# Loads of x in five parts, and bulk loads held back ahead of the rows of maxima, in an attention and MLP kernel

## The chip, the cores and the metric

The kernel runs on one core of a Trainium2 chip. The core has a matrix engine (PE, with its weight loads shown apart as PEld), a vector engine (DVE), a scalar engine (ACT), GpSimd (POOL), and SyncE (SP), which here issues every DMA. The metric is the device time of one execution in microseconds, the median of several runs.

## The reference

```python
H = 32; Dh = D // H; W = 256                      # S = 2048, D = 640, F = 1536
qkv = (x @ wqkv).reshape(B, S, 3, H, Dh)          # heads of 20 columns
scores = einsum("bhqd,bhkd->bhqk", q, k) * Dh ** -0.5
mask = (idx[:, None] - idx[None, :] >= 0) & (idx[:, None] - idx[None, :] < W)
p = softmax(where(mask, scores, -1e9))
s = einsum("bhqk,bhkd->bhqd", p, v) @ wo          # attention branch
h = relu(x @ w1 + b1) ** 2
g = silu(h @ w2 + b2)                             # MLP branch
return x0 + s * g                                 # x = layernorm(x0) feeds both branches
```

All of it is float32. The kernel splits each operand of a product into a high and a low part and adds three products (high by high, high by low, low by high).

## The kernel before

There are three stages. In the first, x is normalised and transposed in four blocks of 512 rows (`BT`), each as a high and a low tile of 128 partitions by 5 x 512 numbers (five column blocks of D). Both tiles of a block are also written to memory (`xs_d`), 1,280 KB each. v and the first group of q and k are computed here.

The second stage is one loop over steps `s` at the end of the kernel, 16 head pairs by 16 tiles of 128 queries and 11 steps more. In each step a pair's scores `sps` are computed and DVE takes their maxima along the rows; nine steps later the transposed scores `stps` of the same tile are computed with the maxima subtracted, and ACT takes their exponential; two steps after that, every fourth step, `values` multiplies by v into `ops`. The maxima travel like this: every fourth step, `max_rows` transposes the maxima of four query tiles, ACT and POOL split them into a high and a low row (`row`, `mrow`), and SP issues two DMAs of 4 KB (`qs<-mrow`) that put them into two rows of the q tile `qs`. The transposed scores read these rows as part of their operand. For three groups of four out of four their first reader comes three steps after the two DMAs, for the first group of a pair five steps.

Between these, PE is filled by a generator (`filler`): first the products for q and k of the other heads (`qkps`), then the MLP in eight blocks, `hps` (x by w1) and `yps` (the squared result by w2), four blocks of x with the first half of F and four with the second. The block order is 3, 0, 1, 2 and then 2, 3, 0, 1, so six of the eight need a new x (`xb`), loaded from `xs_d` by `load_xb` when the last `hps` of the block before is issued. Each `hps` group takes its 30 products for one output column block and half of 512 rows, column block by column block, three products each. Last, the third stage multiplies by wo and writes the output.

The order on every engine is set when the kernel is built, by the code's own clock, with the engines running through their lists in order. PE runs two halves of its rows side by side (`halves`, `both`), the second a little behind the first.

All DMAs stand in SP's one list. They come into it in three ways. Stores (`o<-osb`, `y<-ysb`, `q_d`/`k_d<-shm`) are posted and go out at `post_all`, twice a step. Rows of maxima go out directly. Everything else that is large waits in lists and is handed out by `issue`, twice a step: weight pieces (`start_pieces`, `raw`), and then `bulk`, which holds the loads of q and k for the next head pair (`pair_loads`, eight of 240 KB) and those of x. Each item has a price; each call adds `RATE` = 0.9 of credit, never above 0.9, and items go out while the credit is over zero. `ensure_bulk` issues what has not gone out when its user comes: pair loads at the first step of a pair, x at the start of its block. DMAs use eight completion counters in turn, and one is issued only when the eighth before it has landed.

```python
while credit[0] > 0 and start_pieces(1):
    credit[0] -= 1.0
while bulk and credit[0] > 0:
    cost, fn = bulk.pop(0)
    fn()
    credit[0] -= cost
```

Line numbers in the profile are those of the helper that issues: L681 a bulk DMA, L564 a posted store, L503 a row of maxima, L753 a weight piece, L419 a load of v, L874 a load of `yin` (the first half's y). L468 is a half product, L478 the scores, L518 the transposed scores, L546 `ops`.

## Time and profile before

| | us |
|---|---|
| median of three runs | 883.76 |
| lowest, highest | 883.56, 889.21 |
| the profiled execution | 882.05 |
| its span, first to last instruction | 880.3 |
| stage two (first `load_v` to the last step) | about 116 to 783 |

The page gives busy times by engine, then slices of the span, the DMA queues, the chain of work that ended last, groups of instructions, and DMA issues. Of the queries, "waits" lists who waited for whom, "timeline" lists instructions in order of time (a DMA's row on SP is its issue, not its transfer), and "windows" gives the busy time of each engine in a stretch, with DMA share and GB/s. The granted PE clock is full throughout:

```
PEclk9999999999999999999999999999999999999999
DMA  7997687778788363263366255475255364165995
```

### The profile page before, as it was taken

To read this page: it belongs to the slowest core of one execution; us is meant where nothing else is said; L and a number is where in the kernel's file an instruction comes from. 1 tells how busy PE (TensorE), PEld (TensorE's weight loads), DVE (VectorE), ACT (ScalarE), POOL (GpSimd) and SP (SyncE) were. 2 spreads that over 40 slices of the span, in tenths; PEclk is the share of its full clock that TensorE was granted. 3 is DMA by queue.
4 is the path that set the end of the run, shared out by engine and by line. 5 is a ranking of instruction groups with operands and counts; after the bars stand their busy time and mean duration, and the time that the engine had idled before them with its cause. 6 is when DMAs were issued, how large, how long until landed. Compare 5 with 4: busy or idle time off the path is not lost.

```text
span 880.3 us, 26692 instructions
## 1 busy us (share of the span) xinstructions
PE 860.6 (98%) x10640; PEld 802.6 (91%) x10640; DVE 498.7 (57%) x1448; ACT 414.8 (47%) x800; POOL 329.9 (37%) x700
## 2 busy tenths in 40 slices
PE   8999999999999999999999999999999999999997
PEld 8999999888888899989989989988998989989997
DVE  7652146656567755555555676754655555354774
ACT  5222114545556744744644664743653654642231
POOL 6010002333333643534633543643543543621343
PEclk9999999999999999999999999999999999999999
DMA  7997687778788363263366255475255364165995
GB/s 269 313 394 265 179 230 256 229 249 278 240 269 297 84 223 108 60 224 96 95 207 174 73 154 145 130 223 150 76 202 161 90 209 119 52 196 183 284 299 175
DMA packets 85988, 168.59 MB, mean 192 GB/s; under 512 B 8680, under 2 KB 40552, under 8 KB 83304
## 3 DMA queue, kind: packets, MB, share of 16 engines
q1 hardware_dynamic: 85864, 166.89, 60.1%
q8 instruction: 84, 1.38, 0.7%
q14 instruction: 40, 0.33, 0.1%
HBM read 94.71 MB, written 71.57 MB: 189 GB/s over the span
## 4 chain that ended last, share of the span: by engine, by line
PE 76%; DMA 11%; ACT 4%; DVE 4%; issue 3%; POOL 2%; SPq 0%; DVEq 0%; POOLq 0%; ACTq 0%
PE yps L468 16%; PE hps L468 16%; PE qkps L468 13%; PE ops L546 8%; PE vps L228 8%; DMA qs<-mrow 5%; PE stps L518 4%; PE sps L478 4%; PE qkps L205 3%; DMA out_dram<-res 3%; POOL res L1099 2%; PE wops L599 1%; DMA ks<-k_d 1%; ACT p L524 1%; ACT relu L926 1%
## 5 line engine op out<-in xcount | busy, mean ns | idle before, releaser
L486 DVE CUSTOM_DVE_ANT_0 junk<-sps,mask 128x384 bf16<-128x384 f32 (+2 forms) x512 | 271.9, 531 | 205.0 <-PE sps L478 75.1
L524 ACT ACTIVATE p<-stps 128x768 f32<-128x768 f32 (+2 forms) x256 | 196.9, 769 | 258.0 <-PE stps L518 202.1
L468 PE MATMUL yps<-w,hh 64*128 64x320 f32 x1536 | 231.6, 310 | 4.0 <-DVE sq L931 3.0
L525 POOL TENSOR_SCALAR_AFFINE_SELECT p<-p 128x256 f32<-128x256 f32 x256 | 104.6, 409 | 332.7 <-ACT p L524 327.6
L468 PE MATMUL hps<-xb,w 64*128 64x256 f32 x2520 | 218.2, 283 | 0.0
L468 PEld LDWEIGHTS hps<-xb,w 64*128 64x128 f32 x2520 | 206.4, 187 | 5.2 <-issue 5.1
L468 PEld LDWEIGHTS yps<-w,hh 64*128 64x128 f32 x1536 | 188.8, 185 | 9.7 <-DVE sq L931 4.8
L468 PE MATMUL yps<-w,hl 64*128 64x320 f32 x768 | 182.8, 309 | 0.0
L478 PE MATMUL sps<-ks,qs 60*128 60x384 f32 (+2 forms) x512 | 139.9, 344 | 1.9 <-DVE mt L486 1.6
L518 PE MATMUL stps<-qs,ks 62*128 62x384 f32 (+2 forms) x512 | 130.1, 335 | 5.8 <-DMA qs<-mrow 5.7
L468 PEld LDWEIGHTS yps<-w,hl 64*128 64x128 f32 x768 | 121.6, 185 | 2.1 <-issue 2.1
L468 PE MATMUL qkps<-xT,wgkh 64*128 64x512 f32 x320 | 100.9, 395 | 0.0
L468 PE MATMUL qkps<-xT,wgqh 64*128 64x512 f32 x320 | 99.4, 393 | 0.0
L546 PE MATMUL ops<-p,vp 128*21 128x128 f32 (+1 forms) x2112 | 92.8, 313 | 0.0
L527 POOL TENSOR_SCALAR_AFFINE_SELECT p<-p 128x256 f32<-128x256 f32 x224 | 92.1, 411 | 0.0
L518 PEld LDWEIGHTS stps<-qs,ks 62*128 62x128 f32 x512 | 83.4, 187 | 8.7 <-issue 7.7
L478 PEld LDWEIGHTS sps<-ks,qs 60*128 60x128 f32 x512 | 84.4, 185 | 5.1 <-DVE mt L486 3.9
L546 PEld LDWEIGHTS ops<-p,vp 128*21 128x21 f32 x2112 | 65.2, 100 | 22.3 <-issue 8.8
L932 POOL TENSOR_TENSOR hl<-sq,hh 128x256 fp32r<-128x256 f32 x96 | 70.6, 736 | 27.5 <-DVE sq L931 22.9
L228 PE MATMUL vps<-wv,xT 128*128 128x320 f32 x480 | 71.5, 308 | 0.0
L228 PEld LDWEIGHTS vps<-wv,xT 128*128 128x128 f32 x480 | 70.5, 188 | 0.1
L931 DVE SCALAR_TENSOR_TENSOR sq<-hps,b1t,relu 128x256 f32<-128x256 f32 x96 | 46.2, 482 | 39.2 <-ACT relu L926 39.1
(100 smaller groups left out, 1212.1 us busy)
## 6 DMA issues: line engine op xcount, KB each, us to landing
ks<-k_d SPq DMA_DIRECT2D x64, 240.0 KB
qs<-q_d SPq DMA_DIRECT2D x64, 240.0 KB
xb<-xs SPq DMA_DIRECT2D x12, 1280.0 KB
xs<-xT SPq DMA_DIRECT2D x8, 1280.0 KB
y<-ysb SPq DMA_DIRECT2D x32, 320.0 KB
k_d<-shm SPq DMA_DIRECT2D x19, 512.0 KB
q_d<-shm SPq DMA_DIRECT2D x19, 512.0 KB
o<-osb SPq DMA_DIRECT2D x64, 128.0 KB
```

The source lines that it names most:

```text
L205: nc.tensor.matmul(ps, wt[:, c, :], xT[part][b][:, c * BT + t0:c * BT + t0 + n], start=m == 1, stop=m == 3 * KC)
L228: nc.tensor.matmul(ps, xT[xp][b][:, c * BT + t * P: c * BT + (t + 1) * P], wv[wp][:, c, nh * HALF:(nh + 1) * HALF], start=first and m == 0 ...
L468: return nc.tensor.matmul(out, a[r], b_[r], skip_group_check=True, **kw)
L478: nc.tensor.matmul(ss[hh][:, :nk], qs[i][o, q * P:(q + 1) * P], ks[i][o, k0 * P:k0 * P + nk], start=True, stop=True)
L486: nc.vector.tensor_tensor_reduce(out=junk[:, :nk], in0=ss[hh][:, :nk], in1=mask[:, 3 * P - nk:], scale=1.0, scalar=-3.0e38, op0=ALU.add, o ...
L518: nc.tensor.matmul(tps[:, hh, :n], ks[i][o, kb * P:(kb + 1) * P], qs[i][o, kb * P:kb * P + n], start=True, stop=True)
L524: nc.scalar.activation(p32[:, :, :n], tps[:, :, :n], AF.Exp, scale=SCALE)
L525: nc.gpsimd.affine_select(p32[:, :, 0:P], p32[:, :, 0:P], pattern=[[0, 2], [1, P]], compare_op=ALU.is_ge, fill=0.0, base=0, channel_multip ...
L527: nc.gpsimd.affine_select(p32[:, :, 2 * P:], p32[:, :, 2 * P:], pattern=[[0, 2], [-1, P]], compare_op=ALU.is_gt, fill=0.0, base=0, channel ...
L546: nc.tensor.matmul(ot[r0:r0 + VW, c0:c0 + len(part), :], vps[p][:, kb // 4, kb % 4, hh, :], pt[:, hh, :].rearrange("p (t n) -> p t n", n=P ...
L931: nc.vector.scalar_tensor_tensor(sq, ps.tile[:, sl], b1t[:, fi + i:fi + i + 1], r, ALU.add, ALU.mult)
L932: nc.gpsimd.tensor_sub(hh[1][:, sl], sq, f32(hh[0][:, sl]))
```

## The change

Two things. A load of x for an MLP block is cut into its five column blocks, for each of the two tiles: ten items of 256 KB at a price of 0.8 each instead of two of 1,280 KB at 1.8. And `issue` hands out nothing in a step with `s % 4 == 3`, nor in a step with `s % 4 == 0` until that step's `rows()` has been called. In four steps there are eight calls of `issue`; three of them now do nothing. The gate holds for weight pieces and for pair loads too. Posted stores and loads of v, `yin` and rows of maxima do not pass it, nor does what `ensure_bulk` or `ensure` forces out.

```diff
-    bulk = []
+    bulk, rowed = [], [False]
     credit = [0.0]
 
     def issue(amount):
+        if state[2] % 4 == 3 or state[2] % 4 == 0 and not rowed[0]:
+            return
         credit[0] = min(credit[0] + amount, amount)
...
     def load_xb(b):
         xb = [bigp.tile([P, KC * BT], F32R, tag="big", name=f"xb{p}_{b}") for p in range(2)]
-        its = [bulk_dma(1.8, f32(xb[p]), xs_d[p][b]) for p in range(2)]
+        cs = [slice(c * BT, (c + 1) * BT) for c in range(KC)]
+        its = [bulk_dma(0.8, f32(xb[p])[:, c], xs_d[p][b][:, c]) for p in range(2) for c in cs]
         return xb, its
...
         for s in range(steps):
-            state[2] = s
+            state[2], rowed[0] = s, False
...
             if rows:
                 rows()
+            rowed[0] = True
             fill((s + EARLY_FILL) * pace)
             post_all()
             issue(RATE)
```

The instructions of PE, DVE, ACT and POOL stand in the same order in both programs. SP's list has the 48 issues more, and bulk loads and weight pieces stand at other places in it. One such place, ahead of the MLP block that uses block 1 of x for the first time; before, a load of x on both sides of a row of maxima:

```order
L564 DMA o_87<-osb 2x64x256
L681 DMA xb_1_6149<-xs_1_73 128x2560
L503 DMA qs_116<-mrow 2x4x128 x2
L681 DMA xb_1_6150<-xs_1_77 128x2560
L681 DMA ks_1351<-k_d 60x1024
L681 DMA qs_1350<-q_d 60x1024
```

and now:

```order
L564 DMA o_87<-osb 2x64x256
L503 DMA qs_116<-mrow 2x4x128 x2
L683 DMA xb_1_6157<-xs_1_73 128x512 x5
L683 DMA xb_1_6158<-xs_1_77 128x512
L564 DMA o_88<-osb 2x64x256
L564 DMA y_83<-ysb 128x640
```

The row of maxima now comes first, the two tiles of x in parts behind it, and the loads of k and q later still.

## The prediction

> **What bounds it now.** I read the page first.

> ```profile
> span 880.3 us, 26692 instructions
> PE 860.6 (98%) x10640; PEld 802.6 (91%) x10640; DVE 498.7 (57%) x1448; ACT 414.8 (47%) x800; POOL 329.9 (37%) x700
> ```

> PE is idle for 880.3 - 860.6 = 19.7 us in all, and its program is the same in both kernels. A change in the order of DMAs can give back no more than those idle times that a DMA makes, and can take time only by making new ones. So the next view is the waits of PE, with total, times and longest:

> ```profile
> PE stps L518 <- DMA qs<-mrow: 5.7, 8, 1.7
> ```

> the same for its weight loads, over the whole span,

> ```profile
> PEld stps L518 <- issue: 7.7, 8, 2.0
> ```

> and over 360 to 680 us alone, where most of the loads of x for MLP blocks lie:

> ```profile
> PEld stps L518 <- issue: 6.6, 6, 2.0
> ```

> The transposed scores wait for a row of maxima eight times, 5.7 us as the matmuls show it and 7.7 us as the weight loads do. I use the second, since the pipeline drains before it stands still. Six of the eight, 6.6 us, lie where x is loaded. The longest is read in the chain of waits

> ```profile
> 578.50 10.61 DMA ks<-k_d
> 589.18 6.42 DMA qs<-mrow
> ```

> and on the weight loads' timeline:

> ```profile
> 595.66 0.21 PEld L518 LDWEIGHTS stps<-qs,ks 62*128 62x128 f32 x2 [2.01 <-issue]
> ```

> A 4 KB transfer takes 6.42 us to land, after its issue waited for a load of k that took 10.61 us. What was queued ahead is on SP's timeline:

> ```profile
> 575.22 0.41 SPq L681 DMA_DIRECT2D xb<-xs  x1
> 576.84 1.11 SPq L503 DMA_DIRECT2D qs<-mrow  x2
> 578.06 0.35 SPq L681 DMA_DIRECT2D xb<-xs  x1
> 578.50 0.39 SPq L681 DMA_DIRECT2D ks<-k_d  x1
> ...
> 579.83 0.49 SPq L681 DMA_DIRECT2D qs<-q_d  x1
> 585.25 0.52 SPq L564 DMA_DIRECT2D o<-osb  x1
> 585.87 0.42 SPq L874 DMA_DIRECT2D yin<-y  x1
> 586.35 1.14 SPq L564 DMA_DIRECT2D y<-ysb  x1
> 588.51 1.17 SPq L503 DMA_DIRECT2D qs<-mrow  x2
> ...
> 597.28 0.52 SPq L564 DMA_DIRECT2D o<-osb  x1
> 599.61 1.27 SPq L503 DMA_DIRECT2D qs<-mrow  x2
> ```

> The sizes are in the page's part 6:

> ```profile
> ks<-k_d SPq DMA_DIRECT2D x64, 240.0 KB
> ...
> xb<-xs SPq DMA_DIRECT2D x12, 1280.0 KB
> ...
> y<-ysb SPq DMA_DIRECT2D x32, 320.0 KB
> ...
> o<-osb SPq DMA_DIRECT2D x64, 128.0 KB
> ```

> Two whole loads of x, four loads of k and q, then o, yin and y, and only then the row. Second thing to see: the second row's DMA (589.18) was held until the k load of 578.50 had landed, and that is the eighth DMA ahead of it in program order; SP keeps eight in flight. The last view is the windows; the last two columns are DMA share and GB/s.

> ```profile
> 504.50:507.00 2.50, 2.01 (x29) 1.80 (x28) 1.52 (x5) 1.93 (x6) 2.14 (x5) 1.00 0.13 33
> 583.00:587.50 4.50, 3.89 (x47) 3.83 (x48) 2.60 (x9) 2.10 (x5) 0.93 (x3) 1.00 0.97 248
> 590.00:597.30 7.30, 5.56 (x82) 4.68 (x80) 2.66 (x9) 1.90 (x3) 1.58 (x5) 1.00 0.53 176
> ```

> From 583 to 587.5 us the DMA engines are full at 248 GB/s: the row waits behind bytes. In the first window only an o store moves, at 33 GB/s and a share of 0.13, some 2 of 16 engines; its 128 KB take about 3.9 us, and a row always follows an o store.

> **What the change does, part by part.** *PE, DVE, ACT and POOL* keep their order, instruction for instruction; so the operations cost nothing, and all is in SP's queue. 48 more DMA issues (six blocks by 10 for 2) at 0.41 us each are 20 us of SP, spread over 400 us in which SP mostly waits for data: nothing, except through the slots of eight in flight.

> *The row that follows a load of x.* SP before, around the stall of 2.01 us (xb_3 is x of block 3, ks and qs are the loads of k and q, vp of v, yin of the first half's y; osb, ysb and mrow are stored):

> ```order
> L681 DMA xb_3_10352<-xs_3_75 128x2560
> L503 DMA qs_1350<-mrow 2x4x128 x2
> L681 DMA xb_3_10353<-xs_3_79 128x2560
> L681 DMA ks_117<-k_d 60x1024
> L681 DMA qs_116<-q_d 60x1024
> L681 DMA ks_117<-k_d 60x1024
> L681 DMA qs_116<-q_d 60x1024
> L564 DMA o_88<-osb 2x64x256
> L874 DMA yin<-y_83 128x640
> L564 DMA y_84<-ysb 128x640
> L503 DMA qs_1350<-mrow 2x4x128 x2
> ```

> and now:

> ```order
> L503 DMA qs_1350<-mrow 2x4x128 x2
> L683 DMA xb_3_10376<-xs_3_75 128x512 x5
> L683 DMA xb_3_10377<-xs_3_79 128x512
> L564 DMA o_88<-osb 2x64x256
> L877 DMA yin<-y_83 128x640
> L564 DMA y_84<-ysb 128x640
> L503 DMA qs_1350<-mrow 2x4x128 x2
> ```

> The first row has no load of x ahead of it any more. Ahead of the second stand 6 x 256 = 1,536 KB of bulk where 2 x 1,280 + 4 x 240 = 3,520 KB stood: 2.0 MB less, at 248 GB/s 8.2 us. It was 2.01 us late. This stall goes, and the five like it, for the same move stands at all of them: -6.6 us. What is late next follows.

> *The row after that.* The bulk taken out of the first interval comes in the next. The intervals from the row of 588.51 to that of 599.61, before:

> ```order
> L503 DMA qs_1350<-mrow 2x4x128 x2
> L419 DMA vp_10605<-v_d 128x672
> L874 DMA yin<-y_83 128x640
> L564 DMA y_84<-ysb 128x640
> L564 DMA o_85<-osb 2x64x256
> L503 DMA qs_1350<-mrow 2x4x128 x2
> ```

> and now:

> ```order
> L503 DMA qs_1350<-mrow 2x4x128 x2
> L683 DMA xb_3_10377<-xs_3_79 128x512 x2
> L419 DMA vp_10631<-v_d 128x672
> L683 DMA xb_3_10377<-xs_3_79 128x512 x2
> L683 DMA ks_117<-k_d 60x1024
> L877 DMA yin<-y_83 128x640
> L564 DMA y_84<-ysb 128x640
> L683 DMA qs_116<-q_d 60x1024
> L564 DMA o_85<-osb 2x64x256
> L683 DMA ks_117<-k_d 60x1024
> L683 DMA qs_116<-q_d 60x1024
> L503 DMA qs_1350<-mrow 2x4x128 x2
> ```

> Four parts and four loads of k and q are new, 4 x 256 + 4 x 240 = 1,984 KB: 8.2 us at 248 GB/s. The window of 590 to 597.3 has 0.47 x 7.3 = 3.4 us of DMA time free, so the row lands up to 4.8 us later than now. Its first user is this:

> ```profile
> 605.25 0.19 PEld L518 LDWEIGHTS stps<-qs,ks 62*128 62x128 f32 x1
> ```

> The o store issued at 597.28 is through by about 597.28 + 3.9 = 601.2 at the earliest, the row behind it soon after, so some 3 to 4 us of slack lie before 605.25. Late by 0 to 2 us; I take 1.5, as the two loads behind the o store lie on the same engines. The same interval at its twin, some 200 us before, has no yin load: 0 to 2, I take 0.4.

> *The last part of x.* A load that went out whole is now ten items handed out at about one a turn, five turns in eight. For two of the six blocks the tenth is issued only when the block begins. SP before the sixth such block (xb_0, second time), before:

> ```order
> L503 DMA qs_1350<-mrow 2x4x128 x2
> L874 DMA yin<-y_83 128x640
> L564 DMA y_84<-ysb 128x640
> L419 DMA vp_12259<-v_d 128x672
> ```

> and now:

> ```order
> L503 DMA qs_1350<-mrow 2x4x128 x2
> L877 DMA yin<-y_83 128x640
> L564 DMA y_84<-ysb 128x640
> L683 DMA xb_0_11768<-xs_0_76 128x512
> L683 DMA ks_117<-k_d 60x1024
> ```

> The part takes the place that vp had. On SP's timeline that was here, and for the block of xb_2, where it stands the same way, here:

> ```profile
> 672.87 0.38 SPq L419 DMA_DIRECT2D vp<-v_d  x1
> ```

> ```profile
> 468.83 0.37 SPq L419 DMA_DIRECT2D vp<-v_d  x1
> ```

> The 14th weight load of each block is the first to read the last part (each of the five column blocks takes three products, the last part is the low half of the fifth):

> ```profile
> 673.87 0.19 PEld L468 LDWEIGHTS hps<-xb,w 64*128 64x128 f32 x1
> ```

> ```profile
> 470.31 0.19 PEld L468 LDWEIGHTS hps<-xb,w 64*128 64x128 f32 x1
> ```

> A load of 320 KB with nothing ahead of it, the first of the chain, takes

> ```profile
> 0.80 2.83 DMA xt<-in_A_x_dram
> ```

> Issue plus 2.83 is 675.70 and 471.66: late by 1.8 and 1.35 us. With 640 KB and 320 KB just ahead it is somewhat more: I take 2.3 and 1.7. The other end is the 10.61 us of the k load: late by 9.6 and 9.1. PE takes its instructions in order, so scores queued behind the product wait with it. The other four blocks get their tenth part at least one row of maxima before they begin.

> [...] In the trace the loads of 576 to 580 us went out within 2 us and filled the engines together (share 0.97), so smaller transfers in flight side by side still fill them. [...]

> *Weight loads* pass the same gate. The one that it brings closest to its use, the fifth of w1's second half, stood ahead of this row of maxima and now stands right behind it, at 519.0:

> ```profile
> 517.75 1.27 SPq L503 DMA_DIRECT2D qs<-mrow  x2
> ```

> ACT reads it here:

> ```profile
> 522.19 0.84 ACT L765 ACTIVATE w<-raw 128x768 fp32r<-128x768 f32 x1
> ```

> 519.0 + 2.83 = 521.85: it costs nothing by 0.3 us, and if it lands late some 0.5 us of ACT, which is busy 47% of the span.

> *The stage of q and k* (to 280 us) has the other two stalls, 7.7 - 6.6 = 1.1 us. There the rows stand behind stores of q and k; loads moved from one interval come in the next. I take 0, bounds -1.1 to +2.

> Sum: 882.05 (the profiled execution; its span is 880.3) - 6.6 + 1.5 + 0.4 + 2.3 + 1.7 = 881.35. The median of the three runs, 883.76, lies 1.7 above that execution, so the forecast is **883 us**: old stalls go and nearly as much comes in new places.

> **Rivals.** *A: nothing new is late.* The parts land in time and the next rows too. For it: DMA share 0.53 in the next interval. Against it: the last parts' issue times. 882.05 - 6.6 = 875.5, by the median's offset 877. That is 0.75% faster; over 1% needs 8.8 us, more than all 7.7 us of row stalls, so something beside them would have to go too. Chance 0.22, of it 0.06 over 1%.

> *B: slower, the last part of x.* At the blocks of xb_2 and xb_0 it lands as the k load of 578.50 did, 10.61 us after its issue: 9.6 + 9.1 = 18.7 us; 882.05 - 6.6 + 1.9 + 18.7 = 896, with the offset 898. For it: it is behind yin and y, in slots of eight. Against it: the engines are not behind a large backlog there. It is slower by over 1% once the two stalls and the rows' 1.9 us make 8.8 + 6.6 = 15.4 us, 6.8 us a block. Chance 0.15, of it 0.12 over 1%. [...]

> *C: the rows stay late.* The engines are as full as before and the row sits behind the o store in any case; half of the 6.6 us stays and the new waits are at 2 us each: 882.05 - 3.3 + 8 = 887, with the offset 888.5. Chance 0.15, of it 0.02 over 1%.

> **How the numbers follow.** The likeliest case has the remaining 0.48. A measurement of this kernel tells about 1% from no change. Faster by over 1%: 0.06 (A). Slower: 0.12 + 0.02 = 0.14. Within: 0.80. The range goes from 876, A less the 1.1 us of the first stage, to 890, above C; outside are most of B and the far end of A, under 2 in 10.

> **What would show it.** Waits of the transposed scores for qs<-mrow: the six of 360 to 680 us gone, new ones of 0 to 2 us at the row behind the last parts (near 403 and 603 us). Waits of hps for xb, which the trace of before does not have: two, near 470 and 672 us, of 1.4 to 3 us. PE's idle time: within 3 us of 19.7. I am wrong if hps waits at more than two blocks, if those waits are over 6 us, or if the time moves while PE's idle time does not.

## The result and the profile after

| | before | after |
|---|---|---|
| median, us | 884.40 (20 runs, 880.62 to 889.21) | 889.39 (20 runs, 886.96 to 892.71) |
| ratio of the times, 95% interval | | 1.0055 (1.0040 to 1.0071) |
| profiled execution, us | 882.05 | 892.71 |

The change makes the kernel about 5 us slower, where 883 was forecast. 889.39 lies in the range of 876 to 890, at its upper end, and within the 1% taken for "no change"; but the interval leaves 1 out. The two profiled executions lie near opposite ends of their kernels' runs, so their difference of 10.7 us is twice that of the medians.

The page of the kernel after, head and first part:

```profile
span 891.0 us, 26715 instructions
PE 866.0 (97%) x10640; PEld 806.8 (91%) x10640; DVE 500.5 (56%) x1448; ACT 415.3 (47%) x800; POOL 330.2 (37%) x700
```

Idle time of PE is 891.0 - 866.0 = 25.0 us, 5.3 more than before. But PE's busy time has grown too, by 5.4 us, with the same 10,640 products in the same order. No wait explains that. Its waits, as the matmuls show them (total, times, longest, us):

```profile
PE stps L518 <- DMA qs<-mrow: 5.7, 6, 2.1
PE hps L468 <- DMA xb<-xs: 4.8, 2, 3.3
```

and as the weight loads do:

```profile
PEld stps L518 <- issue: 6.4, 5, 2.3
PEld hps L468 <- DMA xb<-xs: 5.4, 2, 3.6
```

The transposed scores still wait 6.4 us for rows of maxima, where they waited 7.7; the half products wait 5.4 us for x, where they never did. Where, is on the weight loads' timeline (in brackets the idle time ahead, in us):

```profile
193.97 0.22 PEld L518 LDWEIGHTS stps<-qs,ks 62*128 62x128 f32 x2 [0.24 <-issue]
...
225.30 0.21 PEld L518 LDWEIGHTS stps<-qs,ks 62*128 62x128 f32 x2 [1.82 <-issue]
...
346.89 0.21 PEld L518 LDWEIGHTS stps<-qs,ks 62*128 62x128 f32 x2 [0.87 <-issue]
...
406.48 0.21 PEld L518 LDWEIGHTS stps<-qs,ks 62*128 62x128 f32 x2 [1.16 <-issue]
...
475.51 0.18 PEld L468 LDWEIGHTS hps<-xb,w 64*128 64x128 f32 x1 [1.76 <-DMA xb<-xs]
...
610.47 0.22 PEld L518 LDWEIGHTS stps<-qs,ks 62*128 62x128 f32 x2 [2.33 <-issue]
...
682.78 0.18 PEld L468 LDWEIGHTS hps<-xb,w 64*128 64x128 f32 x1 [3.59 <-DMA xb<-xs]
```

None of the six old waits between 360 and 680 us is among them. New are the row behind the last parts, twice (406 and 610 us), the last part of x, twice (475 and 683 us), and one at 347 us that I had not looked for. The row waits at 194 and 225 us were there before, at 0.64 and 0.48 us.

The busy time is explained by windows of 3.41 us around four of these waits (the third column from the end is the granted clock):

```profile
222.81:226.22 3.41, 1.93 (x24) 1.36 (x17) 1.13 (x4) 0.41 (x1) 0.44 (x2) 1.00 0.98 296
226.22:229.64 3.42, 3.42 (x21) 3.27 (x20) 0.57 (x2) 1.41 (x4) 0.77 (x2) 0.50 0.86 265
472.00:475.41 3.41, 2.03 (x29) 1.74 (x25) 2.10 (x7) 1.29 (x2) 1.37 (x4) 1.00 0.81 239
475.41:478.83 3.42, 3.32 (x56) 2.78 (x58) 0.57 (x2) 0.29 (x1) 0.16 (x1) 1.00 1.05 272
608.50:611.91 3.41, 1.41 (x18) 1.44 (x20) 1.10 (x5) 0.93 (x2) 0.05 (x1) 1.00 0.62 163
611.91:615.33 3.42, 3.42 (x32) 3.33 (x30) 1.50 (x5) 1.41 (x4) 1.13 (x4) 0.50 0.11 34
680.19:683.60 3.41, 0.82 (x13) 0.69 (x17) 0.13 (x2) 0.00 (x0) 0.77 (x2) 1.00 1.04 295
683.60:687.01 3.41, 3.41 (x38) 2.38 (x32) 0.00 (x1) 0.00 (x0) 0.00 (x0) 0.50 0.98 224
```

After three of the four waits PE runs at half its clock (0.50) for 3.4 us, which costs up to 3.41 / 2 = 1.7 us each time. The page's slices, tenths of 22 us each, show full clock throughout and hide this. At the longest wait of the kernel before, 2.01 us, the clock stayed:

```profile
591.92:595.33 3.41, 2.03 (x36) 1.31 (x28) 2.01 (x7) 0.22 (x1) 0.77 (x2) 1.00 0.53 163
595.33:598.74 3.41, 3.05 (x41) 3.08 (x43) 0.62 (x5) 1.54 (x3) 0.77 (x2) 1.00 0.30 114
```

The mean granted clock is known of every timed execution, so the time that halvings cost can be compared over runs instead of over two profiles: (1 - clock) x span, called lost clock below. It is 4.7 us in the mean of 20 executions after, and 2.8 us (35 executions) or 1.9 us (17) before, in the runs of before that accompanied the experiments. So some 1.9 to 2.8 of the 5.0 us are clock, and the rest is waits. In the profiles of before and after one more halving begins after the last product has ended (at 878.6 us, the last product at 876.6; at 891.8, the last product at 887.3), so it slows no product. How much of it lies within the span differs (0.9 us of lost clock in the profile before, none after), so it drops out of differences of means only. And the profiled execution of before, with no halving until its last product, is not typical of its kernel: 28 of the 35 executions lost more than 1 us.

### The profile page after: what moved, and what is told of

Its sections match the earlier page's. It is cut to its first block, busy times and chain, and to the rows that moved or that the text cites. A ratio compares the mean times of both kernels' runs of the same rounds, so it can differ in the third digit from the quotient of the medians.

```text
span 891.0 us, 26715 instructions
## 1 busy us (share of the span) xinstructions
PE 866.0 (97%) x10640; PEld 806.8 (91%) x10640; DVE 500.5 (56%) x1448; ACT 415.3 (47%) x800; POOL 330.2 (37%) x700
## 4 chain that ended last, share of the span: by engine, by line
PE 78%; DMA 9%; ACT 3%; DVE 3%; issue 3%; POOL 2%; SPq 1%; DVEq 0%; POOLq 0%; ACTq 0%
PE yps L468 17%; PE hps L468 16%; PE qkps L468 13%; PE ops L546 8%; PE vps L228 8%; PE stps L518 5%; DMA qs<-mrow 4%; PE sps L478 4%; PE wops L599 3%; PE qkps L205 3%; DMA out_dram<-res 2%; DMA xb<-xs 1%; POOL res L1102 1%; DVE sq L934 1%; ACT p L524 1%
## 5 line engine op out<-in xcount | busy, mean ns | idle before, releaser
L468 PE MATMUL yps<-w,hh 64*128 64x320 f32 x1536 | 233.2, 311 | 4.0 <-DVE sq L934 3.0
L468 PE MATMUL hps<-xb,w 64*128 64x256 f32 x2520 | 219.4, 283 | 4.8 <-DMA xb<-xs 4.8
L468 PEld LDWEIGHTS hps<-xb,w 64*128 64x128 f32 x2520 | 207.0, 188 | 10.8 <-DMA xb<-xs 5.4
L468 PEld LDWEIGHTS yps<-w,hh 64*128 64x128 f32 x1536 | 187.8, 185 | 9.6 <-DVE sq L934 4.8
L468 PE MATMUL yps<-w,hl 64*128 64x320 f32 x768 | 181.0, 310 | 0.0
L518 PE MATMUL stps<-qs,ks 62*128 62x384 f32 (+2 forms) x512 | 132.3, 336 | 5.7 <-DMA qs<-mrow 5.7
L468 PEld LDWEIGHTS yps<-w,hl 64*128 64x128 f32 x768 | 119.5, 185 | 2.3 <-issue 2.3
L468 PE MATMUL qkps<-xT,wgkh 64*128 64x512 f32 x320 | 102.1, 399 | 0.0
L468 PE MATMUL qkps<-xT,wgqh 64*128 64x512 f32 x320 | 100.1, 395 | 0.0
L518 PEld LDWEIGHTS stps<-qs,ks 62*128 62x128 f32 x512 | 84.9, 188 | 8.0 <-issue 6.4
## 6 DMA issues: line engine op xcount, KB each, us to landing
xs<-xT SPq DMA_DIRECT2D x8, 1280.0 KB
o<-osb SPq DMA_DIRECT2D x64, 128.0 KB
```

Source lines behind the costliest of these rows:

```text
L468: return nc.tensor.matmul(out, a[r], b_[r], skip_group_check=True, **kw)
L518: nc.tensor.matmul(tps[:, hh, :n], ks[i][o, kb * P:(kb + 1) * P], qs[i][o, kb * P:kb * P + n], start=True, stop=True)
```

## The experiments

The four kernels from "parts, no gate" on ran beside the same 35 executions of before (median 884.38), the last four beside 17 others (885.34); each ratio is against its own, that of the change against 20 more (884.40). Row waits and x waits are the weight loads' waits of `stps` for rows and of `hps` for x in the profiled execution; all in us.

| kernel | median (lowest to highest, runs) | ratio to before, 95% | row waits | x waits | lost clock, mean |
|---|---|---|---|---|---|
| before | 884.38 and 885.34 | 1 | 7.7 | 0 | 2.8 and 1.9 |
| after | 889.39 (886.96 to 892.71, 20) | 1.0055 (1.0040 to 1.0071) | 6.4 | 5.4 | 4.7 |
| parts, no gate | 887.65 (884.58 to 891.37, 12) | 1.0034 (1.0010 to 1.0059) | 11.0 | 0 | 4.7 |
| gate, no parts | 882.71 (879.20 to 886.88, 12) | 0.9967 (0.9944 to 0.9991) | 8.6 | 0 | 2.4 |
| after, parts at 0.36 | 887.91 (882.76 to 893.26, 12) | 1.0030 (1.0001 to 1.0059) | 6.7 | 0 | 5.2 |
| after, o store in two | 882.69 (879.58 to 885.57, 12) | 0.9967 (0.9946 to 0.9988) | 1.7 | 5.4 | 3.3 |
| before, o store in two | 874.37 (873.68 to 875.92, 5) | 0.9881 (0.9857 to 0.9905) | 1.1 | 0 | 0.9 |
| gate, no parts, o store in two | 874.66 (872.12 to 876.83, 6) | 0.9884 (0.9858 to 0.9909) | 0 | 0 | 1.0 |
| after, parts at 0.36, o store in two | 874.79 (873.62 to 878.68, 6) | 0.9890 (0.9864 to 0.9916) | 0 | 0 | 1.3 |
| after, PE kept busy ahead of the late parts | 887.53 (882.01 to 894.54, 12) | 1.0030 (1.0007 to 1.0053) | 5.6 | 1.5 | 3.0 |

### The parts alone

```diff
     def issue(amount):
-        if state[2] % 4 == 3 or state[2] % 4 == 0 and not rowed[0]:
-            return
```

> The change without the gate: x in five parts at 0.8 each, handed out at every call. The last part now goes out before its block begins, so no wait of hps for xb; parts stand ahead of the rows of maxima again. Theory (what costs is where the DMAs stand: late last parts, late rows behind parts, and the clock halved after a long stall): transposed scores wait 5 to 9 us for rows, as before; hps waits 0; no or one halving of the clock outside the end; ratio to before 0.998 to 1.003. [...]

Measured: 887.65 us, 3.3 above before. The waits of this kernel hold no wait of `hps` for x, but more for rows than any other, and more than the 5 to 9 us expected:

```profile
PEld stps L518 <- issue: 11.0, 6, 3.1
```

The ratio of 1.0034 is just above the 1.003 expected, and the profile has two halvings (at 597.2 and 672.3 us) where one at most was expected. The largest wait, 3.14 us, is at 597.5 us. On SP's timeline the row (L503) stands there behind two parts and a load of k:

```profile
588.74 1.89 SPq L681 DMA_DIRECT2D xb<-xs  x2
590.73 0.44 SPq L681 DMA_DIRECT2D ks<-k_d  x1
591.27 1.12 SPq L503 DMA_DIRECT2D qs<-mrow  x2
```

Without the gate ten items spread over several calls of `issue`, and some of them end up right ahead of a row. So the parts at 0.8 cost time without the gate too, and the waits that this profile shows are for rows; the x waits come only with parts and gate together: the gate keeps three calls in eight from handing out parts, and the tenth part falls behind its block.

### The gate alone

```diff
-        cs = [slice(c * BT, (c + 1) * BT) for c in range(KC)]
-        its = [bulk_dma(0.8, f32(xb[p])[:, c], xs_d[p][b][:, c]) for p in range(2) for c in cs]
+        its = [bulk_dma(1.8, f32(xb[p]), xs_d[p][b]) for p in range(2)]
```

> The gate without the parts: x in two whole loads at 1.8 each. Theory: x comes in time (hps waits 0); of the six stalls of 360 to 680 us at most 1.5 us are left (the row behind two whole loads and two pair loads); the row near 222 us is still late by 1.5 to 2 us, since weight and pair loads were moved in front of it; ratio 0.994 to 0.999. Rival (the gate itself costs, by crowding the interval after the rows): rows near 403 and 605 us late by 1 to 2.5 us as in the change, ratio 1.002 to 1.006.

Measured: 882.71 us, 0.33% faster than before, the interval below 1. Half of the change is a gain. But not because the rows are in time. In its profiled execution they wait

```profile
PEld stps L518 <- issue: 8.6, 6, 2.6
```

longer than before (7.7), among other places at 465 us, for 2.6 us. On SP's timeline its row (456.93) now has both whole loads and an o store between it and the row before:

```profile
450.05 0.35 SPq L683 DMA_DIRECT2D xb<-xs  x1
...
450.95 0.38 SPq L683 DMA_DIRECT2D xb<-xs  x1
454.57 0.53 SPq L564 DMA_DIRECT2D o<-osb  x1
456.93 2.97 SPq L503 DMA_DIRECT2D qs<-mrow  x2
```

Of the six old waits two are gone (0.72 us at 382 and 0.87 us at 584 us), those of rows with a load of x on each side. The other four stand at the same rows and come to 6.1 us where they were 5.0, not the 1.5 at most that was expected: two are shorter (0.6 for 1.2 us at 393, 1.1 for 2.0 at 596 us) and two longer (2.6 for 0.6 us at 465, 1.8 for 1.2 at 668 us). The two of the first stage come to 2.5 where they were 1.1. Where the 1.7 us of gain come from is not shown by this profile; lost clock, 2.4 against 2.8, explains little of it.

### The parts at a price at which they are all out in time

```diff
-        its = [bulk_dma(0.8, f32(xb[p])[:, c], xs_d[p][b][:, c]) for p in range(2) for c in cs]
+        its = [bulk_dma(0.36, f32(xb[p])[:, c], xs_d[p][b][:, c]) for p in range(2) for c in cs]
```

> The change with a price of 0.36 a part (ten parts cost what two whole loads cost before). Theory: the parts go out as early as whole loads would, hps waits 0, rows near 403 and 605 us in time; the row near 222 us late by 1.5 to 2 us; ratio 0.994 to 0.999, equal to the gate alone within 0.002. Rival (cutting into parts costs): slower than the gate alone by over 0.003.

Measured: 887.91 us. The waits for x went, as they should when the tenth part goes out as early as the second whole load did. The time did not come down to that of the gate alone; that part of the expectation fell. The rows near 393 and 594 us, expected in time, are 2.4 us late:

```profile
392.90 0.22 PEld L518 LDWEIGHTS stps<-qs,ks 62*128 62x128 f32 x2 [2.37 <-issue]
```

But the gate alone had late rows too, and the two profiles do not show the 5.2 us between the medians: they are 882.76 us (the fastest of its twelve) and 882.91, with 6.7 and 8.6 us of row waits. The clock of the runs shows about half of it: lost clock is the highest of all, 5.2 us, 2.7 more than the gate alone had. Span less lost clock has its median at 880.4 us, against 883.3 for the change: so with the waits for x some 3 us went, and the clock hides part of that. What halved the clock in the slower of these runs no profile shows.

### The o store in two, with the change

Common to all the late rows is an o store just ahead. In the window of 504.5 to 507 us, in the prediction, it moves alone at 33 GB/s on a share of 0.13 of the DMA engines, by estimate two of them (0.13 x 16 = 2.1). Its outer dimension is the two heads of the pair. This edit posts one store per head instead, 64 rows of 1 KB each:

```diff
-            post(o_d[g][:, 2 * p:2 * p + 2, :].rearrange("r h n -> h r n"), osb.rearrange("p e n -> p (e n)"))
+            for hh in range(2):
+                post(o_d[g][:, 2 * p + hh, :], osb[64 * hh:64 * hh + 64].rearrange("p e n -> p (e n)"))
```

> The change with each o store cut in two, one of 64 partitions for each head, so that its outer dimension is 64 and not 2. Theory (a row of maxima is late because it stands behind the o store on two DMA engines): the store takes well under 2 us, the waits for rows fall from 6.4 us of weight loads to under 2; the waits of hps for xb stay at 4 to 6 us with one halving of the clock; ratio 0.997 to 1.001. Rival (rows are late because of bulk bytes alone): waits for rows stay at 5 us or more, ratio 1.004 or more.

Measured: 882.69 us, 6.7 us below the change. Waits:

```profile
PEld hps L468 <- DMA xb<-xs: 5.4, 2, 3.3
PEld stps L518 <- issue: 1.7, 1, 1.7
```

The row waits fall from 6.4 to 1.7 us; those for the last part of x stay at 5.4. So the two are separate causes, and it is the slow store that made most of the rows late. A halving came behind a wait of either kind: of the two halvings of this profile one follows the row wait of 1.7 us (at 604.7 us), the other the longer wait for x (676.4 us). Lost clock is 3.3 us in the mean instead of 4.7.

### The o store in two, without the change

The same edit in the kernel before.

> The kernel before with the o store posted as two DMAs, one per head of the pair, 64 partitions each; loads of x whole, no gate. Theory (the rows of maxima come late because the o store ahead of them sits on some 2 of 16 engines for about 4 us): the weight loads' waits of the transposed scores, 7.7 us in the kernel before, fall below 3 us and the time to 878 to 881. Rival (the rows wait for the bytes of the whole loads ahead of them): the six waits between 360 and 680 us stay, at least 5 us of the 7.7, and the time is within 1.5 us of the kernel before's.

Measured: 874.37 us, 1.2% faster than before, and better than forecast: 3.6 us under the lower end. The waits:

```profile
PEld stps L518 <- issue: 1.1, 2, 0.7
```

The two that are left are at 581 and 591 us, behind the two whole loads and the four of k and q that the prediction shows. In windows of a stretch like that of 504.5 to 507 us before, with the store alone on the engines,

```profile
500.50:501.50 1.00, 0.51 (x7) 0.30 (x6) 0.72 (x2) 0.97 (x3) 0.63 (x2) 1.00 0.56 118
501.50:503.50 2.00, 2.00 (x30) 2.00 (x31) 1.04 (x5) 1.43 (x5) 1.78 (x4) 1.00 0.00 0
```

it moves at 118 GB/s on a share of 0.56 and is through in about 1 us. The six stalls, 6.6 us, that I had put down to 3.5 MB of bulk ahead of a row needed the store at 33 GB/s behind that bulk as well: with the bulk unchanged, 5.5 of the 6.6 us go, and the 1.1 us of the first stage with them. The rival of this run, the bytes alone, holds only for the 1.1 us that are left. Between the profiled executions the gain is 882.05 - 875.92 = 6.1 us, and 7.0 with the lost clock of each taken off (0.9 before, 1.7 here), about as the waits have it. Between the medians it is 11.0: 1.0 is clock (1.9 less 0.9), and the profiled execution of before lies 3.3 us below the median of these 17 runs. It probably waited less than most; no profile here shows one that waited more, so some 3 us of the 11.0 are not assigned. The edit changes two things at once, the number of DMAs and their outer dimension, and no run separates them.

### The o store in two with either half of the change

> The gate alone (loads of x whole) with the o store as two DMAs. Theory: the gate alone was 882.7 with 8.6 us of such waits; they fall below 3 us and the time to 877 to 880, the best of all so far; the gate then adds little to what the two o stores give the kernel before (within 2 us of it). Rival (what is left in the gate alone is the first stage and the bytes of the whole loads): waits above 5 us, time 881 or more.

> The change with the parts at 0.36 each, so that all ten are out well ahead of their block, and the o store as two DMAs. Theory (the two costs of the change are late rows behind the slow o store and late last parts, each with a halved clock behind it): no wait of hps for x, waits of the transposed scores below 3 us, fewer than 2 halvings of the clock an execution, time 878 to 881. Rival (parts cost something of their own, by their number or by SP's eight slots, as the change at 0.36 with the o store whole, 887.9, suggests): above 883 with no wait of hps for x.

Measured: 874.66 and 874.79 us, and the waits of neither profile list one for a row or for x. Both are 2 to 3 us under the lower end of what was expected, and the gate adds as little to the kernel before with the store in two as expected. For the parts, the rival fell: with rows no longer late and all parts in time, 60 loads of 256 KB cost the same as 12 of 1,280 KB, as far as six runs of each tell. So what the parts at 0.36 cost in the third experiment they cost together with the slow store; for the parts without the gate, the first experiment, no run with the store in two was made.

These three are the same within 0.4 us. Once the store is fast, neither the gate nor the parts have anything to gain. The version that beats both kernels is the kernel before with the o store in two.

### PE kept busy ahead of the late parts

```diff
         def front():
+            for _ in range(again):
+                half(0, out, a, b_, start=True, stop=False)
             job.mark = half(0, out, a, b_, start=first, stop=False)
...
-                        halves(job, ps, w_, x_, m == 0, m == len(mms) - 1, i * MT, MT)
+                        halves(job, ps, w_, x_, m == 0, m == len(mms) - 1, i * MT, MT, {3: 14, 6: 24}.get(n, 0) * (m + th + fp == 0))
```

> The change, with work that nobody needs put on PE ahead of the two late last parts: the first product of the first half product of a block is done 14 times more at the block of xb_2 near 475 us and 24 times more at that of xb_0 near 683 us (0.12 us each, 1.7 and 2.9 us), each time overwritten. So PE computes while it would have stood still, and the last part of x lands no sooner. Theory (PE standing still for 1.5 us and more is what halves its clock for the next 3.4 us): the two waits fall from 1.8 and 3.6 us to below 1 us, no halving at 683 us, 0.7 to 1 halving an execution less than the change's 2.7 (mean clock 0.9962 instead of 0.9947), time 887 to 888. Rival (the halving has another cause, as a transfer or a load step when PE starts again at any time): halvings as in the change, time 889 to 890.

Measured: 887.53 us, 1.9 below the change, with 38 products more. The weight loads' timeline at the two places:

```profile
472.37 0.18 PEld L468 LDWEIGHTS hps<-xb,w 64*128 64x128 f32 x1 [0.64 <-DMA xb<-xs]
```

```profile
677.37 0.18 PEld L468 LDWEIGHTS hps<-xb,w 64*128 64x128 f32 x1 [0.90 <-DMA xb<-xs]
```

The waits are below 1 us, the trace has no halving near 680 us, and lost clock falls from 4.7 to 3.0 us in the mean of 12 executions, the length of one halving. Span less lost clock stays (883.0 against 883.3), as it should when products take the place of waiting. The waits, the clock and the time are as the theory had them, and not as the rival had them (time and clock unchanged). How much the work gained is less sure: the two ratios' intervals overlap, and before itself lost 2.8 us in one set of runs and 1.9 in the other, so up to 1.0 of the 1.7 us may lie in the set.

## Why the prediction was wrong

**The six old stalls, -6.6 us: right in effect, half wrong in cause.** All six are gone. But they were not due to the bytes alone. The prediction said "the row waits behind bytes" and noted in the same paragraph that the o store uses some 2 of 16 engines and that a row always follows it; it did not put the two together. With the bytes left in place and the store in two, 5.5 of the 6.6 us went as well: the rows were late by both together, and either one taken away is enough for most of it.

**The row after that, +1.5 and +0.4: mis-sized.** "Late by 0 to 2 us; I take 1.5" measured 2.33 us near 610, and 0.4 measured 1.16 near 406. The interval was filled as worked out; SP's timeline and the windows after it:

```profile
600.11 0.53 SPq L564 DMA_DIRECT2D o<-osb  x1
600.68 0.50 SPq L683 DMA_DIRECT2D ks<-k_d  x1
601.23 0.55 SPq L683 DMA_DIRECT2D qs<-q_d  x1
602.43 1.29 SPq L503 DMA_DIRECT2D qs<-mrow  x2
```

```profile
598.82:602.43 3.61, 3.61 (x53) 3.61 (x52) 1.99 (x9) 2.35 (x5) 1.21 (x4) 1.00 0.99 284
...
606.00:610.47 4.47, 2.44 (x50) 1.65 (x46) 1.86 (x8) 0.74 (x1) 0.77 (x2) 1.00 0.91 268
```

The row needs 8 us from its issue to its user, with the engines full at 0.91 and more all the while. That fits the 4.8 us worked out as the upper end, if the slack was some 2.5 us (4.8 - 2.33) and not the 3 to 4 that I had allowed; I then took a value near the middle of a range whose upper end had the argument (bytes and free DMA time) behind it.

**The last part of x, +2.3 and +1.7: the place right at both blocks, one size off.** Near 475 us 1.76 was measured for 1.7. Near 683 us it was 3.59 for 2.3. SP's timeline there:

```profile
678.22 0.42 SPq L683 DMA_DIRECT2D xb<-xs  x1
678.74 0.45 SPq L683 DMA_DIRECT2D ks<-k_d  x1
679.23 0.47 SPq L683 DMA_DIRECT2D qs<-q_d  x1
679.80 0.39 SPq L419 DMA_DIRECT2D vp<-v_d  x1
680.24 0.43 SPq L683 DMA_DIRECT2D ks<-k_d  x1
680.71 0.40 SPq L683 DMA_DIRECT2D qs<-q_d  x1
```

The part took 682.78 - 678.22 = 4.56 us to be there, where I took 2.83 from a load with nothing ahead of it and added about half a microsecond for what is ahead. Five loads come right behind it, and the engines are full while PE waits (a share of 1.04 in the window of 680.19 to 683.60; a packet counts in the window in which it starts, so a share can pass 1). At 475 us, where as many loads come right behind it, it took 3.21; what SP's list has more at 683 us is the yin load of 320 KB ahead of it. No run changed that alone. The 10.61 us of rival B did not happen.

**The first stage, 0: inside its bounds, not zero.** 0.24 and 1.82 us are 2.1 where 1.1 was, and the second brought a halving. It does not always do so: the last experiment's kernel waited 1.81 us there with no halving, and the kernel with the parts at 0.36, with the same SP list up to there, waited 0.62 us. The wait at 347 us, 0.87 us, was not in the sum. It is one more row behind moved bulk: SP's list has two parts and four loads of k and q between that row and the one before, where it had a store of y, and with the o store in two the wait is gone.

**What was missing: the clock.** This is the step that failed: "can take time only by making new ones", new idle times, and so a sum that counts each stall as its own length and a PE busy time taken as fixed. It grew by 5.4 us. Summed with the measured lengths, its terms give -7.7 + 6.4 + 5.4 = +4.1 us for the profiled execution instead of -0.7; its three halvings add 3 x 1.7 = 5.1 us, as PE's busy time has it (before, the only one came after the last product); 9.2 in all, and the other 1.5 of the 10.7 us are not assigned. Fewer long stalls can cost more than many short ones: in the profile before, six stalls of 0.6 to 2.0 us and no halving among them (other executions of it had some); after, one of 1.8, one of 2.3 and one of 3.6, each with one. Over all runs, span less lost clock has its median at 880.5 us before (35 executions) and 883.3 after: 2.8 us of the 5.0 are waits and about 2 are clock.

**The range, and rival C.** That 889.39 lies in the range is no merit of the sum: C set its upper end. C's 888.5 came from half of the old row waits staying and four new waits of 2 us. The four new ones came to 8.8 us, where the sum had 5.9, but none of the six old ones stayed, and the clock made up for them; that the figure is near is in good part luck. A did not happen, since new waits came; of B the place came true, with 1.8 and 3.6 us in place of 9.1 and 9.6.

**The tests named in advance.** The six stalls gone: yes. New ones near 403 and 603 of 0 to 2 us: there, one larger. Two `hps` waits of 1.4 to 3 us: at both places and no other, one larger. PE's idle time within 3 us of 19.7: missed, 25.0. "If the time moves while PE's idle time does not" was the right alarm for the other half: PE's busy time moved by 5.4.

**The size of the parts, no cost of its own.** The prediction took from the row of 0.97 that smaller transfers in flight side by side still fill the engines. The runs agree: 874.79 us with 256 KB parts and 874.66 with whole loads, both with the store in two.

## What to carry to other kernels

Ahead of a small transfer that is late, look not only for the most bytes but for the transfer that moves at the lowest rate and DMA share: with megabytes of bulk left ahead of the 4 KB rows, 128 KB posted as two DMAs that moved at 118 GB/s and 0.56 instead of one at 33 GB/s and 0.13 took away 6.6 of 7.7 us of waits. Cost a stall of PE as its length plus, from about 1.7 us on (the shortest that a halving followed here, but for four halvings whose cause stays open), a chance of half a clock for 3.4 us. Several short stalls may then be cheaper than a long one, which no run here tested by itself; PE kept busy through a stall was. Read the mean clock of every run, since slices of 22 us do not show it. When loads are cut into more items at a fixed rate of handing out, work out when the last item goes out, and with what right behind it.

## What the runs showed of the hardware

| busy share of a window | windows | followed by half clock |
|---|---|---|
| under 0.5 | 5 | 5 |
| 0.53 to 0.6 | 4 | 2 |
| 0.6 to 0.65 | 6 | 0 |
| over 0.65 | 2,139 | 4 |

Of the four at the foot three are windows of 0.80 at the start of the third stage, where PE's work is another, and one is of 0.69 at 506.6 us in the kernel before with the store in two; busy time alone does not decide there, and the cause of these four stays open. So a wait of 2.0 us that fell across two windows cost nothing more (before, 591.92 to 598.74 us: 2.03 / 3.41 = 0.60, the clock stays at 1.00), and one of 1.82 us that lay within one window (after, ahead of 225.30 us: 1.93 / 3.41 = 0.57) was followed by 3.41 us at 0.50, by estimate 1.7 us. But for the four at the foot, the shortest waits that a halving followed were 1.7 to 1.8 us. The lost clock of single executions comes mostly in steps of about 1.8 us, one halving each: 1.8 to 7.1 us in 20 runs of the kernel after. Part of the spread of the times goes with it: the correlation of time and lost clock is 0.57 in these 20 runs and 0.91 in the 35 of before. As the grid begins at another place in each of the three profiles above, where a wait falls in it is a likely part of it; no run shows that by itself.

**The o store moved at 33 GB/s as one DMA and at 118 as two:** a share of 0.13 of 16 engines, by estimate two of them, for 128 KB as one DMA whose outer dimension is 2, and 0.56 as two DMAs of 64 rows, with 11 us of the kernel's time between them. Two DMAs of the first kind side by side would by estimate make 2 x 0.13 = 0.26, so their number alone does not explain it. Which engines a transfer uses is not in these traces; that the row waits on the same engines as the store is my inference and was not shown.
